# One hand-ordered schedule for block-sparse attention and a gated layer: passes of 256 queries, plain loads and DMA transposes in place of TensorE transposes

## The chip, the cores and the metric

The kernel runs on one core of one Trainium2 chip. The metric is the device time of one execution in microseconds (us), the median of three runs. Times of single instructions are from one execution taken by the hardware profiler. The engines are named as in the profile: PE is TensorE (PEld its weight loads), DVE is VectorE, ACT is ScalarE, POOL is GpSimd, SP is the queue engine that here only issues DMAs.

## The reference

Attention over 4 batches, 8 heads, 768 positions and 64 features per head, with a mask in blocks of 32 positions (24 by 24 blocks: the neighbours, the first and last rows and columns, and three sampled blocks in each row). The result, 3,072 rows of 512, goes through one layer: a product to 1,024 columns, h times softmax(h), a normalisation by mean and variance with gain, and a product back to 512 columns.

```python
scores = scale * np.matmul(q, k.transpose(0, 1, 3, 2))
...  # mask of 32 x 32 blocks, masked scores -> -1e9
attn = np.exp(scores - np.max(scores, axis=-1, keepdims=True))
attn = attn / (np.sum(attn, axis=-1, keepdims=True) + 1e-09)
x = np.matmul(attn, v)        # then (B, S, H * D) -> 3072 x 512
h = x @ w_in                  # 3072 x 1024
e = np.exp(h - np.max(h, axis=-1, keepdims=True))
solu = h * e / (np.sum(e, axis=-1, keepdims=True) + 1e-09)
mu, var = np.mean(solu, -1, keepdims=True), np.var(solu, -1, keepdims=True)
out = ((solu - mu) / np.sqrt(var + 1e-06) * g_ln) @ w_out
```

## The kernel before

**Attention.** The work goes in 16 pairs of heads. A pair has 9 units; a unit is 1,024 columns of scores (keys on the partitions, queries along the columns), which PE writes into two banks of PSUM and one ACT instruction turns into bf16 exponentials (`score_unit`). 16 times 9 gives 144 units. The mask needs no instruction of its own: `kT128` and `qT128` are 128 rows tall, 64 of them features, 24 more a factorised mask, so that the score product adds a large negative number where a block is masked. The exponentials of a pair are kept, and one pair later `out_mms` multiplies them with `vaug` (V and a column of ones, 65 columns): 72 products a pair, 8 a unit. `normalise` divides by the last column and writes `xb`, the rows of the layer's input.

**Loads and transposes.** `load_head` issues three DMAs on POOL's queue for a head, each turning fp32 into bf16 on the way. `transpose_head` brings Q and K of a head into the transposed form: 6 PE transposes into one PSUM bank, one DVE copy into `kT128` or `qT128`; two heads a pair.

**The layer.** It goes in 24 tiles of 128 rows. A tile has five steps (`moe_step`): `moe_x` (4 PE transposes, a DVE copy), `moe_h` twice (4 products of 512 columns, exponential on ACT, product and statistics on DVE), `moe_t` for the tile before (8 PE transposes, a DVE copy) and `moe_o` for the tile before (8 products, scaling on ACT, the store). One step in six is empty.

**The order.** Program order is only a priority; a scheduler places the instructions on each engine. A tile can start when all 8 heads of its batch are done, so steps are issued only from the sixth pair on (`p > PB`), one a unit. The steps left when the last pair is done run alone (the `while` loop). Transposes of Q and K, of `moe_x` and of `moe_t` share one PSUM buffer, `p_tp`. The weights are loaded at the start; `prep_w`, `prep_mean` and the subtraction fold gain and mean into `w_cen_sb`.

Of the kernel before, what the change touches and what calls it, by code (L numbers as in the profile page):

```python
# [7 lines left out]
FP32 = mybir.dt.float32  # L8
# [193 lines left out]
def kernel(  # L202
# [15 lines left out]
    NB = S // BLK  # L218
    TQ = 128
# [11 lines left out]

    nc.scalar.preload_act_table_set("natural_log_exp_and_others")

    const_pool = ctx.enter_context(tc.tile_pool(name="const", bufs=1))

    qT128 = [const_pool.tile([TQ, S], BF16, name=f"qT128_{i}") for i in range(2)]
    kT128 = [const_pool.tile([TQ, S], BF16, name=f"kT128_{i}") for i in range(2)]
    for t in qT128 + kT128:
        nc.vector.memset(t[D : TQ, :], 0.0)

    with tc.tile_pool(name="m_ps", bufs=1, space=bass.MemoryType.PSUM) as m_ps, \
         tc.tile_pool(name="m_sb", bufs=1) as m_sb:
        maskT = block_mask(nc, m_sb, m_ps, sampled_blocks, NB, NEG)

        sel = m_sb.tile([NB, NB, BLK], FP32)
        nc.vector.memset(sel, 0.0)
        nc.gpsimd.affine_select(out=sel, in_=sel, compare_op=ALU.not_equal,
                                fill=1.0, base=0, channel_multiplier=1,
                                pattern=[[-1, NB], [0, BLK]])
        for t in kT128:  # L250
            nc.vector.tensor_copy(out=t[D : D + NB, :].rearrange("p (q o) -> p q o", o=BLK),
                                  in_=sel)
        for t in qT128:
            nc.vector.tensor_copy(out=t[D : D + NB, :].rearrange("p (q o) -> p q o", o=BLK),
                                  in_=maskT.rearrange("p (q o) -> p q o", o=1).broadcast_to([NB, NB, BLK]))

    ident = const_pool.tile([128, 128], BF16)
    nc.vector.memset(ident, 0.0)
    nc.gpsimd.affine_select(out=ident, in_=ident, compare_op=ALU.not_equal,
                            fill=1.0, base=0, channel_multiplier=1,  # L260
                            pattern=[[-1, 128]])
    mean_w = const_pool.tile([128, 128], BF16)
    nc.vector.memset(mean_w, 1.0 / d_ff)


    recip_all = const_pool.tile([TQ, B * H * NCH], FP32)
    esum_all = const_pool.tile([128, n_tiles * 2], FP32)
    n_r, n_e = B * H * NCH, n_tiles * 2
# [5 lines left out]
    nc.vector.memset(ones_c, 1.0)  # L274

    w_in_sb = const_pool.tile([128, KD, d_ff], BF16)
    w_out_sb = const_pool.tile([128, KF, d_model], BF16)
    w_cen_sb = const_pool.tile([128, KF, d_model], BF16)
    g_ln_sb = const_pool.tile([128, KF], FP32)
    w_out_f = const_pool.tile([128, KF, d_model], FP32)  # L280

    work = ctx.enter_context(ExitStack())
    a_qk = work.enter_context(tc.tile_pool(name="a_qk", bufs=4))
    a_exp = work.enter_context(tc.tile_pool(name="a_exp", bufs=2))
# [4 lines left out]
    p_tp = work.enter_context(tc.tile_pool(name="p_tp", bufs=1, space=bass.MemoryType.PSUM))  # L289
    p_h = work.enter_context(tc.tile_pool(name="p_h", bufs=2, space=bass.MemoryType.PSUM))  # L290

    xbs = {}
    loads = {}

    def load_head(bi):
        b, h = bi // H, bi % H
        qc = a_qk.tile([TQ, NCH, D], BF16, tag="qc")
        kc = a_qk.tile([TQ, NCH, D], BF16, tag="kc")
        nc.gpsimd.dma_start(out=kc, in_=k[b, h, :, :].rearrange("(c p) d -> p c d", p=TQ))  # L299
        nc.gpsimd.dma_start(out=qc, in_=q[b, h, :, :].rearrange("(c p) d -> p c d", p=TQ))  # L300
        vaug = a_qk.tile([TQ, NCH, D + 1], BF16, tag="vaug")
        nc.gpsimd.dma_start(  # L302
            out=vaug[:, :, 0:D],
            in_=v[b, h, :, :].rearrange("(c p) d -> p c d", p=TQ))
        nc.vector.memset(vaug[:, :, D : D + 1], 1.0)
        loads[bi] = (qc, kc, vaug)

    def transpose_head(bi):
        qc, kc, _ = loads[bi]
        for src, dst in ((kc, kT128[bi % 2]), (qc, qT128[bi % 2])):  # L310
            tp = p_tp.tile([D, S], BF16, tag="tp")
            for c in range(NCH):
                nc.tensor.matmul(tp[:, c * TQ : (c + 1) * TQ],  # L313
                                 src[:, c, :], ident, is_transpose=True,
                                 start=(c == 0), stop=(c == NCH - 1))
            nc.vector.tensor_copy(out=dst[0:D, :], in_=tp)  # L316
# [3 lines left out]
    UNITS = 9  # L320
    exs_of = {}

    def score_unit(pair, u):
        if u == 0:
            exs_of[pair] = a_exp.tile([TQ, 2 * NCH * S], BF16, tag="exs", name=f"exs{pair}")
        sco = p_sco.tile([TQ, 2, 512], FP32, tag="sco")
        for i in range(2):
            bank = 2 * u + i
            bi = 2 * pair + bank // 9
            lo = (bank % 9) * 512  # L330
            hi = lo + 512
            c = lo
            while c < hi:
                jc = c // S
                e = min(hi, (jc + 1) * S)
                nc.tensor.matmul(sco[:, i, c - lo : e - lo],  # L336
                                 kT128[bi % 2][:, jc * TQ : (jc + 1) * TQ],
                                 qT128[bi % 2][:, c - jc * S : e - jc * S],
                                 start=(c == lo), stop=(e == hi))
                c = e  # L340
        nc.scalar.activation(out=exs_of[pair][:, u * 1024 : (u + 1) * 1024],  # L341
                             in_=sco.rearrange("p a b -> p (a b)"), func=ACT.Exp, scale=scale)

    ops_of = {}

    def out_mms(pair, i0, i1):

        for i in range(i0, i1):
            hh, jc, ic = i // 36, (i % 36) // NCH, i % NCH
            bi = 2 * pair + hh  # L350
            if i % 36 == 0:
                ops_of[bi] = p_op.tile([TQ, NCH, D + 1], FP32, tag="op", name=f"op{bi}")
            op = ops_of[bi]
            base = hh * NCH * S + jc * S + ic * TQ
            nc.tensor.matmul(op[:, ic, :], exs_of[pair][:, base : base + TQ],  # L355
                             loads[bi][2][:, jc, :],
                             start=(i % 36 == 0), stop=(i % 36 == 35),
                             skip_group_check=True)
            if i % 36 == 35:
                normalise(bi, op)  # L360

    def normalise(bi, op):
        b, h = bi // H, bi % H
        if h == 0:
            xbs[b] = a_sm.tile([TQ, NCH, H * D], BF16, tag="xb", name=f"xb{b}")
        recip = recip_all[:, bi * NCH : (bi + 1) * NCH].rearrange("p (c o) -> p c o", o=1)
        nc.vector.reciprocal(out=recip, in_=op[:, :, D : D + 1])
        nc.vector.tensor_tensor(out=xbs[b][:, :, h * D : (h + 1) * D], in0=op[:, :, 0:D],  # L368
                                in1=recip.broadcast_to([TQ, NCH, D]), op=ALU.mult)


    xTs, solus, rstds = {}, {}, {}

    def moe_x(t):
        xb = xbs[t // NCH]
        tps = p_tp.tile([128, KD, 128], BF16, tag="tp")
        for c in range(KD):
            nc.tensor.matmul(tps[:, c, :], xb[:, t % NCH, c * 128 : (c + 1) * 128],  # L378
                             ident, is_transpose=True,
                             start=(c == 0), stop=(c == KD - 1))  # L380
        xTs[t] = mo_sb.tile([128, KD, 128], BF16, tag="xT", name=f"xT{t}")
        nc.vector.tensor_copy(out=xTs[t], in_=tps)  # L382

    stats_of = {}

    def moe_h(t, i):
        xT = xTs[t]
        if i == 0:
            solus[t] = mo_sb.tile([128, d_ff], BF16, tag="solu", name=f"solu{t}")
            stats_of[t] = mo_sb.tile([128, 2, 6], FP32, tag="stats", name=f"stats{t}")  # L390
        hps = p_h.tile([128, HF], FP32, tag="h")
        for c in range(KD):
            nc.tensor.matmul(hps, xT[:, c, :], w_in_sb[:, c, i * HF : (i + 1) * HF],  # L393
                             start=(c == 0), stop=(c == KD - 1))
        e = mo_sb.tile([128, HF], BF16, tag="e")
        nc.scalar.activation(out=e, in_=hps, func=ACT.Exp, scale=1.0,  # L396
                             accum_out=esum_all[:, 2 * t + i : 2 * t + i + 1])
        so = solus[t][:, i * HF : (i + 1) * HF]
        nc.vector.tensor_mul(out=so, in0=hps, in1=e)  # L399
        nc.vector.bn_stats(out=stats_of[t][:, i, :], in_=so)  # L400
        if i == 1:
# [12 lines left out]
            nc.scalar.activation(out=rstds[t], in_=lnv, func=ACT.Exp, scale=-0.5)  # L414

    lnTs = {}

    def moe_t(t):
        tps2 = p_tp.tile([128, KF, 128], BF16, tag="tp")
        for c in range(KF):  # L420
# [135 lines left out]
```

## Time and profile before

| what | value |
|---|---|
| median of 3 runs (lowest, highest) | 303.93 us (303.35, 303.96) |
| span of the profiled execution, first to last instruction | 302.5 us |
| busy: PE, DVE, ACT, POOL | 248.4, 165.1, 195.7, 82.7 us |
| mean granted TensorE clock | 0.982 |
| HBM read, written | 23.07 MB, 6.29 MB |

The page gives no time of the profiled execution but its span, which is 1.43 us below the median of the runs; whoever adds up durations of the profile gets a span, and has to add that much for a time. "Busy" is the time in which an engine had an instruction under way. PE's instructions overlap, so its rate is read from the distance of two starts and not from the length of one instruction. In lists of groups, the number behind the x is a count, and the last part is the idle time of the engine ahead of these instructions with what ended it. The stages of the kernel are read from the view of windows, which gives the busy time of each engine in a stretch of the span.

### The profile page before, as it was taken

The numbers are of one execution on the slowest core, as the hardware profiler recorded it, in microseconds if no ns is written. First come the engines' busy times: TensorE is split into PE (matmuls) and PEld (weight loads), VectorE is DVE, ScalarE is ACT, GpSimd is POOL, SyncE is SP. The second block draws the span as 40 slices with busy tenths as digits, with TensorE's granted clock in tenths as the row PEclk, the third lists the DMA queues.
The fourth block names the chain that finished last, engine by engine and source line by source line (L and its number), as shares of the span: only waits on it lengthen the run. The fifth ranks groups of instructions, "written<-read, shape, count | busy, mean of one in ns | idle before, by whom it ended". The sixth has DMA issues, their size and how long they took to land.

```text
span 302.5 us, 6313 instructions
## 1 busy us (share of the span) xinstructions
PE 248.4 (82%) x2556; PEld 152.2 (50%) x2603; DVE 165.1 (55%) x446; ACT 195.7 (65%) x315; POOL 82.7 (27%) x110
## 2 busy tenths in 40 slices
PE   0248999998989898979989999699889987777772
PEld 0024666665655465545656655465545564333430
DVE  6263343434567356357466556547456756757770
ACT  1005999997868586838768776759857863344340
POOL 5069655543424232323333242232111000000000
PEclk9999999999999999979999999989999999999997
DMA  5989999997647664765946774756213011011002
GB/s 150 264 55 120 91 68 71 62 67 52 42 28 78 72 73 30 76 39 63 89 39 63 74 77 26 76 62 48 44 41 22 35 37 37 35 66 41 36 35 78
DMA packets 81365, 19.35 MB, mean 64 GB/s; under 512 B 76721, under 2 KB 76722, under 8 KB 81330
## 3 DMA queue, kind: packets, MB, share of 16 engines
q0 software_dynamic: 75792, 10.49, 51.1%
q1 hardware_dynamic: 5538, 8.39, 7.9%
q8 instruction: 22, 0.36, 0.5%
q14 instruction: 13, 0.11, 0.1%
HBM read 23.07 MB, written 6.29 MB: 97 GB/s over the span
## 4 chain that ended last, share of the span: by engine, by line
PE 49%; DVE 24%; ACT 12%; issue 8%; DMA 5%; POOL 1%; SPq 0%; DVEq 0%; ACTq 0%
PE sco L336 12%; PE ops L430 10%; DVE solu L399 8%; PE tp L313 8%; PE hps L393 8%; PE op L355 7%; ACT exs L341 6%; ACT e L396 5%; DVE stats L400 5%; DMA w_out_f<-in_moe_w_out_dram 4%; DVE lnT L425 3%; DVE qT L316 2%; PE tps L421 1%; PE tps L378 1%; ACT ot L433 1%
## 5 line engine op out<-in xcount | busy, mean ns | idle before, releaser
L341 ACT ACTIVATE exs<-sco 128x1024 bf16<-128x1024 f32 x144 | 141.2, 1027 | 20.8 <-PE sco L336 13.3
L336 PE MATMUL sco<-qT,kT 128*128 128x256 bf16 (+1 forms) x354 | 86.2, 331 | 2.6 <-ACT exs L341 1.1
L355 PEld LDWEIGHTS <-exs 128*128 128x128 bf16 x1152 | 52.9, 99 | 20.7 <-DVE xb L368 4.1
L355 PE MATMUL op<-vaug,exs 128*128 128x65 bf16 x1152 | 60.7, 195 | 2.1 <-issue 0.8
L430 PE MATMUL ops<-w_cen_sb,lnT 128*128 128x512 bf16 x186 | 46.9, 384 | 7.5 <-DVE lnT L425 6.0
L393 PE MATMUL hps<-w_in_sb,xT 128*128 128x512 bf16 x181 | 45.6, 380 | 5.9 <-DVE xT L382 4.4
L399 DVE TENSOR_TENSOR solu<-hps,e 128x512 bf16<-128x512 f32 x48 | 32.7, 682 | 27.2 <-ACT e L396 27.2
L299 POOL DMA_DIRECT2D kc<-in_k_dram x32 | 26.7, 833 | 75.2 <-PE tp L313 64.0
L336 PEld LDWEIGHTS <-kT 128*128 128x128 bf16 x384 | 32.0, 99 | 17.4 <-issue 4.2
L433 ACT ACTIVATE ot<-ops,rstd 128x512 f32<-128x512 f32 x24 | 16.5, 687 | 37.3 <-PE ops L430 19.8
L396 ACT ACTIVATE e<-hps 128x512 bf16<-128x512 f32 x48 | 28.8, 601 | 17.0 <-PE hps L393 16.4
L302 POOL DMA_DIRECT2D vaug<-in_v_dram x32 | 26.5, 829 | 45.4 <-PE op L355 34.3
L400 DVE BATCH_NORM_STATS2 stats<-solu 128x6 f32<-128x512 bf16 x48 | 32.9, 685 | 10.5 <-issue 6.6
L300 POOL DMA_DIRECT2D qc<-in_q_dram x32 | 26.7, 835 | 25.1 <-PE tp L313 12.1
L430 PEld LDWEIGHTS <-lnT 128*128 128x128 bf16 x192 | 16.8, 99 | 26.6 <-DVE lnT L425 9.6
L316 DVE COPY qT<-tp 64x768 bf16<-64x768 bf16 x32 | 17.3, 539 | 21.2 <-PE tp L313 19.7
L393 PEld LDWEIGHTS <-xT 128*128 128x128 bf16 x192 | 15.9, 97 | 22.0 <-DVE xT L382 7.1
L316 DVE COPY kT<-tp 64x768 bf16<-64x768 bf16 x32 | 17.3, 541 | 15.4 <-PE tp L313 8.1
L313 PE MATMUL tp<-ident,kc 128*64 128x128 bf16 x192 | 18.0, 228 | 7.7 <-DVE lnT L425 3.7
L313 PE MATMUL tp<-ident,qc 128*64 128x128 bf16 x192 | 17.4, 228 | 6.9 <-DVE kT L316 6.4
L313 PEld LDWEIGHTS <-kc 128*64 128x64 bf16 x192 | 12.8, 112 | 18.0 <-issue 16.9
L313 PEld LDWEIGHTS <-qc 128*64 128x64 bf16 x192 | 12.6, 112 | 16.9 <-issue 15.6
(62 smaller groups left out, 159.5 us busy)
## 6 DMA issues: line engine op xcount, KB each, us to landing
out_dram<-ot SPq DMA_DIRECT2D x24, 256.0 KB, 2.0
kc<-in_k_dram POOLq DMA_DIRECT2D x32, 96.0 KB, 3.0
qc<-in_q_dram POOLq DMA_DIRECT2D x32, 96.0 KB, 3.0
vaug<-in_v_dram POOLq DMA_DIRECT2D x32, 96.0 KB, 3.2
w_out_f<-in_moe_w_out_dram SPq DMA_DIRECT2D x1, 2048.0 KB, 11.0
w_in_sb<-in_moe_w_in_dram POOLq DMA_DIRECT2D x1, 1024.0 KB, 10.7
samp_i<-in_sampled_blocks_dram SPq DMA_DIRECT2D x1, 0.6 KB
g_ln_sb<-in_moe_g_ln_dram SPq DMA_DIRECT2D x1, 4.0 KB, 2.4
```

What stands on the lines that cost most here:

```text
L299: nc.gpsimd.dma_start(out=kc, in_=k[b, h, :, :].rearrange("(c p) d -> p c d", p=TQ))
L300: nc.gpsimd.dma_start(out=qc, in_=q[b, h, :, :].rearrange("(c p) d -> p c d", p=TQ))
L313: nc.tensor.matmul(tp[:, c * TQ : (c + 1) * TQ], src[:, c, :], ident, is_transpose=True, start=(c == 0), stop=(c == NCH - 1))
L316: nc.vector.tensor_copy(out=dst[0:D, :], in_=tp)
L336: nc.tensor.matmul(sco[:, i, c - lo : e - lo], kT128[bi % 2][:, jc * TQ : (jc + 1) * TQ], qT128[bi % 2][:, c - jc * S : e - jc * S], start ...
L341: nc.scalar.activation(out=exs_of[pair][:, u * 1024 : (u + 1) * 1024], in_=sco.rearrange("p a b -> p (a b)"), func=ACT.Exp, scale=scale)
L355: nc.tensor.matmul(op[:, ic, :], exs_of[pair][:, base : base + TQ], loads[bi][2][:, jc, :], start=(i % 36 == 0), stop=(i % 36 == 35), skip ...
L393: nc.tensor.matmul(hps, xT[:, c, :], w_in_sb[:, c, i * HF : (i + 1) * HF], start=(c == 0), stop=(c == KD - 1))
L396: nc.scalar.activation(out=e, in_=hps, func=ACT.Exp, scale=1.0, accum_out=esum_all[:, 2 * t + i : 2 * t + i + 1])
L399: nc.vector.tensor_mul(out=so, in0=hps, in1=e)
L400: nc.vector.bn_stats(out=stats_of[t][:, i, :], in_=so)
L430: nc.tensor.matmul(ops, lnTs[t][:, c, :], w_cen_sb[:, c, :], start=(c == 0), stop=(c == KF - 1))
```

## The change

The program is written anew between the start and the final check, inside `manual_schedule()`: the order in which instructions are written down is now the order of each engine. Every step goes into a list with a time in units (`at(when, fn, ...)`), and `emit` writes the list in the order of these times.

- A pass is 256 queries of one batch with all 8 heads: 12 passes of 12 units, again 144 units of 1,024 columns. A unit is two heads by two tiles of keys by 256 queries: 4 score products of 256 columns (before: 2 or 3 products of 512 or 256), one exponential, and 8 products with V one and a half units later.
- A pass is all that two tiles of the layer need, so the layer of a pass runs in the pass after it, cut into pieces of 2 or 3 products of 512 columns, one piece a unit.
- Rows are dealt out as `(p c)`: a partition holds 6 successive positions, so Q, K, V come in plain fp32 DMAs of two heads with 1,536 bytes in a row, issued on SP (three of the first on ACT). The cast to bf16 is an instruction of POOL (46 of 48) or DVE (2).
- The mask's 24 rows are written as columns 64 to 87 of the natural-layout tiles `kn` and `qn` once, and are transposed with them; the score product then has 88 rows instead of 128.
- Q and K of the first batch are transposed on PE (`turn_pe`, 96 transposes); of the other three by DMA (`turn_dma`: 24 DMAs of 12 blocks of 128 by 128). The layer's input (`x_turn`, 12 DMAs of 8 blocks) and its inner activation (`ln_turn`, 24 DMAs of 8 blocks) are transposed by DMA only. All are issued on SP.
- The exponential of the layer is one instruction of 1,024 columns, the inverse root is a power on POOL, the last scaling is on DVE.

```diff
-    def load_head(bi):
-        nc.gpsimd.dma_start(out=kc, in_=k[b, h, :, :].rearrange("(c p) d -> p c d", p=TQ))
...
-    def transpose_head(bi):
-    def moe_x(t):
-    def moe_t(t):
...
+    def at(when, fn, *args):
+        plan.append((when, len(plan), fn, args))
+    def emit():
+        for _, _, fn, args in sorted(plan, key=lambda x: x[:2]):
+            fn(*args)
...
+    def load(eng, src, b, pr, key):
+        st = a_st.tile([TQ, 2, NCH * D], FP32, tag="st", name=f"st_{key}{b}_{pr}")
+        eng.dma_start(out=st, in_=src[b, 2 * pr : 2 * pr + 2].rearrange(
+            "h (p c) d -> p h (c d)", c=NCH))
+    def turn_dma(b, pr, key):
+        src, dst = (kn, KT[b % 2]) if key == "k" else (qn, QT[b % 2])
+        nc.sync.dma_start_transpose(
+            out=dst[:, 2 * NCH * pr : 2 * NCH * (pr + 1), :],
+            in_=src[:, 2 * pr : 2 * pr + 2].rearrange("p h c e -> p (h c e)"))
...
+    def x_turn(ps):
+        xT_of[ps] = mo_sb.tile([128, PC * KD, 128], BF16, tag="xT", name=f"xT{ps}")
+        nc.sync.dma_start_transpose(out=xT_of[ps],
+                                    in_=xb_of.pop(ps).rearrange("p c m -> p (c m)"))
+    def ln_turn(ps, i):
+        lnT_of[ps, i] = mo_sb.tile([128, KF, 128], BF16, tag="lnT", name=f"lnT{t}")
+        nc.sync.dma_start_transpose(out=lnT_of[ps, i], in_=solu_of[ps, i])
...
+    with tc.manual_schedule():
...
+        for s in range(n_units):
+            at(s, exps, s)
+            at(s + 1.5, outs, s)
+            if s + 2 < n_units:
+                at(s + 0.8, scores, s + 2)
+            if u == UP - 1:
+                at(s + 1.55, normalise, ps, pr)
+        for b in range(1, B):
+            s0 = SLOTS * NPB * (b - 1) + (14 if b == 1 else 2)
...
+                    at(s0 + 1.5 * n, load, nc.sync, src, b, pr, key)
+                    at(s0 + 1.5 * n + 3.0, cast, nc.gpsimd, b, pr, key)
+                    if key != "v":
+                        at(s0 + 1.5 * n + 4.5, turn_dma, b, pr, key)
+        for ps in range(NPASS):
+            b0 = SLOTS * (ps + 1)
+            at(b0 + 0.6, x_turn, ps)
+            for i in range(PC):
+                hs = b0 + 3 + 6 * i
+                at(hs + 0.1, h_mms, ps, i, 0, 3)
+                at(hs + 1.1, h_mms, ps, i, 3, 6)
+                at(hs + 2.1, h_mms, ps, i, 6, 8)
+                at(hs + 2.95, e_exp, ps, i)
+                at(hs + 3.9, solu, ps, i)
+                at(hs + 3.92, ln_turn, ps, i)
+                at(hs + 4.0, stats, ps, i)
+                at(hs + 5.0, rstd, ps, i)
+                os = hs + 9
+                at(os + 0.1, o_mms, ps, i, 0, 3)
+                at(os + 1.1, o_mms, ps, i, 3, 6)
+                at(os + 2.1, o_mms, ps, i, 6, 8)
+                at(os + 2.9, store, ps, i)
```

More of the change, by code (lines that the diff above doesn't have):

```diff
@@ L230 @@
     n_tiles = n_tok // 128
+    KR = D + NB
+    PC = 2
+    QW = PC * TQ
+    NPB = NCH // PC
+    NPASS = B * NPB
+    NP = H // 2
+    UP = NCH // 2
+    SLOTS = NP * UP
     nc.scalar.preload_act_table_set("natural_log_exp_and_others")
     const_pool = ctx.enter_context(tc.tile_pool(name="const", bufs=1))
[L236 to L255, printed above, removed]
     ident = const_pool.tile([128, 128], BF16)
[L258 to L261, printed above, removed]
     mean_w = const_pool.tile([128, 128], BF16)
[L263 to L268, printed above, removed]
+    n_r, n_e = NPASS * NP * 4, n_tiles
+    recip_all = const_pool.tile([TQ, n_r], FP32)
+    esum_all = const_pool.tile([128, n_tiles], FP32)
     okr = const_pool.tile([128, n_r + n_e], FP32)
@@ L323, in score_unit @@
-    def score_unit(pair, u):
-        if u == 0:
[L325 to L360, printed above, removed]
```

455 lines of the change are left out of this document (296 added, 159 removed).

## The prediction

> **What bounds the kernel now.** I read the page first (busy times, slices, chain), then the windows, then the timeline of PE, then the groups.
>
> ```profile
> PE 248.4 (82%) x2556; PEld 152.2 (50%) x2603; DVE 165.1 (55%) x446; ACT 195.7 (65%) x315; POOL 82.7 (27%) x110
> PE   0248999998989898979989999699889987777772
> ACT  1005999997868586838768776759857863344340
> ```
>
> PE is nearly always busy from the fifth slice on, but ACT is full only in slices 5 to 9, and PE falls to 7 and below in the last seven. So there are stages. I cut the span at the first exponential, at the first step of the layer, and at the end of the last attention exponential:
>
> ```profile
> 24.94 1.94 ACT L341 ACTIVATE exs<-sco 128x1024 bf16<-128x1024 f32 x2 [6.29 <-PE sco L336]
> ...
> 245.95 1.02 ACT L341 ACTIVATE exs<-sco 128x1024 bf16<-128x1024 f32 x1
> ```
>
> ```profile
> 0.00:24.90 24.90, 6.64 (x25) 3.13 (x26) 13.49 (x40) 2.08 (x3) 11.31 (x24) 1.00 0.92 153
> 24.90:67.20 42.30, 41.29 (x505) 26.91 (x513) 16.19 (x44) 40.77 (x44) 26.02 (x33) 1.00 1.23 79
> 67.20:247.00 179.80, 162.99 (x1743) 102.14 (x1772) 101.28 (x271) 134.00 (x215) 45.39 (x56) 0.98 0.55 54
> 247.00:302.50 55.50, 37.51 (x294) 20.02 (x297) 34.13 (x93) 18.88 (x55) 0.00 (x0) 0.97 0.12 45
> ```
>
> Columns: length, then busy time of PE, PEld, DVE, ACT, POOL, the granted clock, DMA share, GB/s. A head of 24.9 us with hardly any product; 42.3 us of attention alone (45 of the 144 units), ACT full; 179.8 us of 99 units with one layer step each, 1.816 us a unit; a tail of 55.5 us in which layer tiles run one behind the other. The distance of two stores' scalings in the tail is one tile, 5.83 us:
>
> ```profile
> 264.23 0.69 ACT L433 ACTIVATE ot<-ops,rstd 128x512 f32<-128x512 f32 x1 [2.50 <-issue]
> ...
> 270.06 0.69 ACT L433 ACTIVATE ot<-ops,rstd 128x512 f32<-128x512 f32 x1 [2.50 <-issue]
> ```
>
> **PE's prices**, from the distance of starts in its timeline:
>
> ```profile
> 160.90 0.52 PE L313 MATMUL tp<-ident,kc 128*64 128x128 bf16 x6
> 161.36 0.42 PE L355 MATMUL op<-vaug,exs 128*128 128x65 bf16 x8
> 161.61 0.59 PE L336 MATMUL sco<-qT,kT 128*128 128x512 bf16 x2
> 162.04 0.41 PE L355 MATMUL op<-vaug,exs 128*128 128x65 bf16 x8
> ...
> 164.31 0.61 PE L421 MATMUL tps<-ident,solu 128*128 128x128 bf16 x8 [0.19 <-DVE qT L316]
> 164.75 0.60 PE L336 MATMUL sco<-qT,kT 128*128 128x512 bf16 x3
> ...
> 165.70 1.90 PE L430 MATMUL ops<-w_cen_sb,lnT 128*128 128x512 bf16 x8
> 167.44 0.39 PE L378 MATMUL tps<-ident,xb 128*128 128x128 bf16 x4
> ```
>
> Six transposes of Q or K take 0.46 us (77 ns each), eight products with V 0.25 (31 ns), one unit's scores 0.43, eight transposes of the layer 0.44 (55 ns), eight products of 512 columns 1.74 (0.217). A unit of the 99 holds 0.43 + 0.25 + 24/9 x 0.077 + 2 x 0.055 + 24/9 x 0.217 = 1.58 us. It takes 1.816, so 0.24 is waiting. In that stage PE is the bound; the transposes are 0.315 of it.
>
> **PE after the change.** A unit keeps its scores (1,024 columns; now four products with a weight load each, where a load with a 65-column product takes 31 ns altogether, so a load hides under 108 ns of columns; 88 rows instead of 128 I price at nothing, the columns being as many), its 8 products with V, and 32/12 products of the layer: 0.44 + 0.25 + 0.58 = 1.27 us, 15.2 a pass. All transposes but 96 leave PE, and with them the DVE copies and the one PSUM buffer that three kinds shared.
>
> **The other engines as the next bound.**
>
> ```profile
> 29.23 31.17 ACT L341 ACTIVATE exs<-sco 128x1024 bf16<-128x1024 f32 x33 [0.73 <-PE sco L336]
> ```
>
> ```profile
> L341 ACT ACTIVATE exs<-sco 128x1024 bf16<-128x1024 f32 x144 | 141.2, 1027 | 20.8 <-PE sco L336 13.3 <-PE tp L313 6.8
> L396 ACT ACTIVATION_READ_ACCUMULATOR e<-hps 128x1 f32 x48 | 9.6, 200 | 0.0
> L399 DVE TENSOR_TENSOR solu<-hps,e 128x512 bf16<-128x512 f32 x48 | 32.7, 682 | 27.2 <-ACT e L396 27.2
> L368 DVE TENSOR_TENSOR xb<-op,recip_all 128x384 bf16<-128x384 f32 x32 | 17.7, 554 | 0.8
> L433 ACT ACTIVATE ot<-ops,rstd 128x512 f32<-128x512 f32 x24 | 16.5, 687 | 37.3 <-PE ops L430 19.8 <-issue 17.5
> L247 POOL TENSOR_SCALAR_AFFINE_SELECT sel<-sel 24x768 f32<-24x768 f32 x1 | 1.0, 987 | 0.7 <-DVE ident L258 0.7
> ```
>
> Undisturbed, 33 exponentials take 31.17 us: 0.945 each. ACT then has 12 x 0.945 + 2 x (1.03 + 0.20) = 13.8 us a pass, below 15.2: it follows PE, with 1.4 to spare. DVE takes over the scaling (at most the 16.5 us of ACT) and loses its copies; even without losing them it would have 182 us. POOL loses its DMA issues and gets 46 casts of 768 columns. The nearest row is the select of 768 columns, 0.99 us: 46 us in all, hidden as long as a cast is ready 1.5 units before its transpose; at double the price still hidden, since the next batch is loaded a batch ahead.
>
> **The DMA transposes** appear in no trace of before, and they decide. 36 + 24 DMAs move 24 x 12 + 36 x 8 = 576 blocks of 128 x 128 bf16, all on SP's queue with 45 loads and 24 stores. Nearest rows:
>
> ```profile
> q0 software_dynamic: 75792, 10.49, 51.1%
> q1 hardware_dynamic: 5538, 8.39, 7.9%
> ...
> out_dram<-ot SPq DMA_DIRECT2D x24, 256.0 KB, 2.0
> w_out_f<-in_moe_w_out_dram SPq DMA_DIRECT2D x1, 2048.0 KB, 11.0
> ```
>
> A packet of q0 costs 302.5 x 16 x 0.511 / 75,792 = 32.6 ns for 138 bytes on average, one of q1 69 ns for 1,515 bytes. Lower bound: a transpose is an ordinary copy of 256 KB, 2.0 us from issue to landing like the store. Upper bound of the rows: 138 bytes a packet, 0.48 us a block over 16 engines, 3.9 + 2.0 = 5.9 us. I take rows of 256 bytes (one row of a block) at q0's price: 128 x 32.6 ns / 16 = 0.26 us a block, 2.1 + 2.0 = 4.1 us for 8 blocks. It lies between the ends and is nearest to small packets, which a transpose has to cut.
>
> Against these rows stands a rule: the Trainium skill, in "VectorE: DVE Perf Modes", § The three transpose paths, puts a 128 x 128 block at 1309 ns by DMA and 390 ns on TensorE; the trace disagrees with the second, with 55 ns in a stream, and cannot show the first. The Trainium skill, in "DMA: Bandwidth & Descriptors", § Latency and other measured facts, measured 261 GB/s for DMA transposes, an estimated 0.126 us a block; by this page the sum below would be about 235.
>
> Where the landing counts: `x_turn` follows the last `normalise` of a pass, and the layer's first product stands in PE's fixed order at b0 + 3.1. Between that pass's last products and it PE has three units of scores, two of products with V and two pieces of the layer: 3 x 0.44 + 2 x 0.25 + 5 x 0.217 = 2.9 us. `normalise` takes some 0.9 of that (L368 and its reciprocal). So 2.0 us of cover, and PE stands 2.1 us a pass; behind it wait products with V and scores, then ACT. On SP, loads and transposes of the next batch wait behind `x_turn`, and nobody needs them within 14 units. `ln_turn` has four units or more (5 us): hidden. The long exponential of the layer delays the next unit's by 1.23 us, of which ACT's spare time and the second score buffer take most: 0 to 1.23, I take 0.3, twice a pass. Pass: 15.2 + 2.1 + 0.6 = 17.9 us, or 1.49 a unit; the present 0.24 us of waiting a unit would give 1.51, about the same.
>
> **Head.** Now the mask is done at 15.26 and K's load leaves at 17.52:
>
> ```profile
> 15.26 0.17 DVE L53 TENSOR_TENSOR maskT<-maskT,anyeq 24x24 f32<-24x24 f32 x1
> ...
> 17.52 0.84 POOL L299 DMA_DIRECT2D kc<-in_k_dram  x1 [10.17 <-DVE w_out_sb L451]
> ...
> 20.62 0.82 PE L313 MATMUL tp<-ident,kc 128*64 128x128 bf16 x6 [2.59 <-DMA kc<-in_k_dram]
> ```
>
> Both came late behind the weights. After: Q and K of two heads, 0.8 MB, at w_out's rate (2 MB in 11 us) land by 6 us. The mask's selects (two of 768 columns and ten short ones), memsets and factors take an estimated 11.7; then 4.3 us from transpose to first exponential as now (20.62 to 24.94): 16. Bounds: 6 + 4.3 = 10, and 24.9 as now.
>
> **First pass,** without a layer: ACT's pace, 12 x 0.945 = 11.3, and 1.2 for late transposes: 12.5. Top: 12 x 1.8 = 22.
>
> **Tail,** one pass of the layer alone, after the last exponential: products with V and `normalise` 0.9, transpose 4.1, h 1.74, exponential 1.23, product with e 2 x 0.68 = 1.36, the same three for the second tile (one h buffer) 4.33, transpose 4.1, out 1.74, scaling 0.68, store 2.3: 22.5 us. It was 55.5.
>
> **Sum:** 16 + 12.5 + 11 x 17.9 + 22.5 = 248; 302.5 becomes 248. The runs' median is 1.4 above the span, so 249.
>
> **The rivals.**
> *Transposes like ordinary copies* (2.0 us): no wait for `x_turn`, 15.8 a pass, tail 18.3: 16 + 12.5 + 174 + 18.3 + 1.4 = 222. For it: the store's 2.0. Against: small pieces. Chance 0.22.
> *Landing of about 6 us and over*, queueing included: 3.9 us of standing, 19.7 a pass, tail 26: 273, up to 300 where `x_turn` waits behind loads or turns of the next batch. Chance 0.15.
> *SP's queue becomes the bound; slower.* A pass brings 48 blocks and on average 5.9 us of loads and stores (48 loads of 256 packets and 4,150 packets of stores at 69 ns over 16 engines). At 0.48 us a block that is 29 us a pass, 11 x 29 + 51 + 1.4 = 373. It decides from (302.5 - 51) / 11 = 22.9 us a pass, 0.35 us a block. For it: 0.26 is not far below, and already gives the DMA engines 18.4 us a pass, as much as a pass lasts. Against: a transpose whose packets carry more than 256 bytes is far from it. By the Trainium skill's 1309 ns ("VectorE: DVE Perf Modes", § The three transpose paths), block after block, an estimated 754 us in transposes alone. Chance 0.19.
> *The change doesn't do what it says*: the transposes moved but PE's fixed order gives back as waits what they took, 1.8 us a unit: 51 + 132 x 1.8 + 1.4 = 290, and 308 with head and first pass at their tops; it alone can end within 0.2% of now (about what a measurement of this kernel can tell). Chance of that 0.01.
>
> **How the numbers follow.** The forecast's own case has 0.43 and reaches from 235 to 262. Faster in all but the third rival and the equal case: 0.80; same 0.01; slower 0.19. The range goes from the copy-like case, 222, to 303, which leaves out the slower case and little below.
>
> **What would show it.** Right: about 60 transposes on SP landing in 3 to 5 us; PE waiting about 2 us for `x_turn` once a pass and for nothing else as long; the distance of 12 exponentials about 18 us; the first exponential near 16; about 22 us after the last. Wrong: DMA engines busy all along with SP's transposes landing in over 8 us (queue bound), PE waiting for casts of POOL or for `normalise` in every group, or an ACT that is full (then PE's prices were too high).

## The result and the profile after

The changed kernel takes 278.89 us (median of 5 runs, 275.16 to 282.94) against 303.96 before (303.35 to 304.99), a ratio of 0.9095 (95% interval 0.9039 to 0.9151; the ratio is of the undisturbed runs, 275.16 to 278.89). It is faster by 9 per cent, where the forecast's own case, 249.0, was 18; its range, 222 to 303, holds the result, the 235 to 262 of its own case does not. The profiled execution has a span of 276.8 us; the prediction's sum for the span was 248.

From the page: busy times, slices of PE, of the granted clock and of the DMA engines, the hardware queue, and the chain by engine.

```profile
span 276.8 us, 5494 instructions
PE 211.5 (76%) x2191; PEld 143.7 (52%) x2224; DVE 134.4 (49%) x317; ACT 169.2 (61%) x195; POOL 63.8 (23%) x100
PE   0699795768989519969989907997989989895752
PEclk9999999968999956997999975999999999999997
DMA  7799587999899999980369999993351233553441
...
q1 hardware_dynamic: 93460, 44.97, 70.0%
...
PE 45%; DMA 23%; DVE 12%; ACT 8%; SPq 4%; issue 4%; POOL 2%; POOLq 0%; DVEq 0%; ACTq 0%
```

PE lost 36.9 us of busy time, but its slices have two holes in mid-kernel (a 1 and a 0) where there were none before. At each hole and in the slice behind it the granted clock falls to 5 to 7 tenths. Around each hole the DMA engines stand at 9 for several slices; before they had 0.55 in this stage. DMA now carries 23 per cent of the chain.

The waits of PE, with total, count and longest:

```profile
PE h L406 <- DMA xT<-xb: 29.4, 12, 8.3
PE sco L349 <- ACT exs L360: 9.8, 20, 0.5
...
PE o L455 <- DMA lnT<-solu: 4.9, 4, 2.5
PE op L373 <- DVE xb L387: 3.1, 2, 2.4
```

One wait dominates, the layer's first product for `x_turn`: 29.4 us in 12 passes, but 8.3 us in the worst. It is not one constant a pass. So the passes have to be looked at one by one. Cut at every twelfth exponential, the passes from the second on take 20.3, 22.9, 17.2, 27.8, 20.4, 17.2, 27.3, 18.0, 17.1, 17.2 and 15.4 us. The first pass, four of these and the tail in the view of windows (columns as in the prediction):

```profile
13.90:29.80 15.90, 15.32 (x208) 13.35 (x207) 8.27 (x18) 11.80 (x12) 7.24 (x11) 1.00 1.02 281
...
73.00:90.20 17.20, 15.20 (x172) 10.49 (x173) 9.45 (x22) 13.81 (x19) 3.81 (x6) 1.00 0.91 185
90.20:118.00 27.80, 18.34 (x176) 12.18 (x180) 9.47 (x22) 13.92 (x18) 8.18 (x11) 0.82 1.14 264
118.00:138.40 20.40, 17.14 (x175) 11.55 (x177) 9.47 (x22) 13.81 (x18) 1.09 (x2) 0.92 0.40 74
...
200.90:218.00 17.10, 15.52 (x175) 10.84 (x177) 9.47 (x22) 13.84 (x18) 1.10 (x2) 1.00 0.33 78
...
250.60:276.80 26.20, 13.28 (x67) 5.22 (x65) 13.90 (x33) 3.34 (x6) 1.64 (x3) 0.91 0.35 91
```

The row from 200.9 is the pass as it was forecast: no loads, PE busy 15.52 us of 17.10. The row from 90.2 does the same work for PE and ACT in 27.80 us. It is a pass in which the next batch is loaded (POOL has 11 instructions, nearly all casts), the DMA share is 1.14, and the clock 0.82. The next row has no loads left (share 0.40) and is long all the same, with the clock at 0.92; the experiment without loads comes back to it.

The stages together: the 144 units took 42.3 + 179.8 = 222.1 us before and take 15.9 + 220.8 = 236.7 now, though 20 of the 24 tiles of the layer end in them instead of 15. The head is 11.0 us shorter and the tail 29.3. So the whole gain stands in the head and the tail; the stage in which the transposes were to be saved, which the prediction put at 209.4, became longer.

What happened at the start of the long pass, in the order of SP's queue, and PE's row behind it:

```profile
91.88 2.55 SPq L312 DMA_TRANSPOSE KT<-kn  x1
94.48 0.58 SPq L297 DMA_DIRECT2D st_k<-in_k_dram  x1
95.35 1.68 SPq L312 DMA_TRANSPOSE QT<-qn  x1
97.08 0.57 SPq L297 DMA_DIRECT2D st_q<-in_q_dram  x1
97.75 2.29 SPq L398 DMA_TRANSPOSE xT<-xb  x1
100.14 1.63 SPq L426 DMA_TRANSPOSE lnT<-solu  x1
...
102.95 1.46 PE L406 MATMUL h<-w_in_sb,xT 128*128 128x512 bf16 x3 [8.13 <-DMA xT<-xb]
```

`normalise` ended at 92.60, but SP was busy until 97.65 with two transposes and two loads for the next batch, which nobody needs for many units. `x_turn` left 5.15 us late; its first product came another 5.21 us later, where a quiet pass has 0.03 and 3.27. PE stood for 8.13 us. Then it ran at half clock: three products of 512 columns took 1.46 us, where the same three take 0.81 to 0.82 at full clock.

```profile
97.90:108.00 10.10, 5.04 (x30) 2.96 (x31) 0.60 (x2) 1.02 (x1) 2.99 (x4) 0.50 1.14 252
```

By the clock's records in the trace, half clock lasted 6.8, 10.2, 3.4 and 10.2 us in the four stretches between the first pass and the tail. The Trainium skill, in "TensorE: Matmul & The Clock Gate", Part 1, says that PE's clock falls to half after an idle window of 3,413 ns and comes back after a busy one; the four durations are one, two and three such windows, so the trace agrees in the lengths. It also shows that such a window need not be idle throughout. The stretches of half clock start at 56.85, 97.81, 125.12, 162.66 and 268.48, whole multiples of 3.413 us apart. Three stretches of that length, the first two right before half clock:

```profile
94.40:97.81 3.41, 0.42 (x4) 0.13 (x2) 1.76 (x6) 1.44 (x2) 1.66 (x2) 1.00 1.12 291
121.70:125.12 3.42, 1.37 (x16) 0.72 (x15) 1.08 (x4) 1.45 (x2) 0.55 (x1) 1.00 1.11 161
251.41:254.82 3.41, 1.80 (x15) 0.84 (x14) 2.36 (x5) 0.56 (x2) 0.00 (x0) 1.00 0.17 34
```

PE was busy 1.37 of 3.42 us in the second, with one wait of 2.05, and the clock fell; it was busy 1.80 of 3.41 in the third, and the clock stayed, though a wait of 3.08 us (253.21 to 256.30) began there. Laid over this trace from its first clock record on, the windows at full clock with PE busy for at most 0.40 of them are followed by half clock, those with 0.53 or more are not.

The landings (median us from issue to landing):

```profile
out_dram<-ot SPq DMA_DIRECT2D x24, 256.0 KB, 2.6
...
lnT<-solu SPq DMA_TRANSPOSE x24, 3.5
xT<-xb SPq DMA_TRANSPOSE x12, 3.2
KT<-kn SPq DMA_TRANSPOSE x12, 5.0
QT<-qn SPq DMA_TRANSPOSE x12, 5.0
```

### The profile page after: what moved, and what is told of

It reads as the page before. It is cut to its first block, busy times and chain, and to the rows that moved or that the text cites. A ratio compares the mean times of both kernels' runs of the same rounds, so it can differ in the third digit from the quotient of the medians.

```text
span 276.8 us, 5494 instructions
## 1 busy us (share of the span) xinstructions
PE 211.5 (76%) x2191; PEld 143.7 (52%) x2224; DVE 134.4 (49%) x317; ACT 169.2 (61%) x195; POOL 63.8 (23%) x100
## 2 busy tenths in 40 slices
DMA packets 94834, 47.60 MB, mean 172 GB/s; under 512 B 77908, under 2 KB 90196, under 8 KB 94804
## 4 chain that ended last, share of the span: by engine, by line
PE 45%; DMA 23%; DVE 12%; ACT 8%; SPq 4%; issue 4%; POOL 2%; POOLq 0%; DVEq 0%; ACTq 0%
DMA xT<-xb 15%; PE h L406 14%; PE sco L349 14%; PE op L373 8%; PE o L455 7%; ACT e L413 4%; ACT exs L360 4%; DMA st_v<-in_v_dram 3%; DVE solu L419 3%; DMA lnT<-solu 3%; SPq L312 2%; DVE stats L433 2%; DMA st_q<-in_q_dram 2%; PE tp_q L323 1%; DVE xb L387 1%
## 5 line engine op out<-in xcount | busy, mean ns | idle before, releaser
L349 PE MATMUL sco<-QT,KT 88*128 88x256 bf16 x576 | 91.8, 283 | 10.8 <-ACT exs L360 9.8
L406 PE MATMUL h<-w_in_sb,xT 128*128 128x512 bf16 x170 | 54.9, 412 | 31.5 <-DMA xT<-xb 29.4
L373 PE MATMUL op<-VA,exs 128*128 128x65 bf16 x1152 | 61.6, 197 | 3.1 <-DVE xb L387 3.1
L349 PEld LDWEIGHTS <-KT 88*128 88x128 bf16 x576 | 50.3, 101 | 18.7 <-issue 13.5
L455 PE MATMUL o<-w_cen_sb,lnT 128*128 128x512 bf16 x181 | 51.2, 389 | 5.6 <-DMA lnT<-solu 4.9
L413 ACT ACTIVATE e<-h 128x1024 bf16<-128x1024 f32 x24 | 24.6, 1023 | 33.3 <-PE h L406 33.3
L448 POOL TENSOR_TENSOR rstd<-vpe,mhalf 128x1 f32<-128x1 f32 x24 | 13.3, 553 | 120.8 <-DVE vpe L441 120.7
L419 DVE TENSOR_TENSOR solu<-h,e 128x1024 bf16<-128x1024 f32 x24 | 29.1, 1214 | 3.4 <-ACT e L413 3.4
L387 DVE TENSOR_TENSOR xb<-op,recip_all 128x256 bf16<-128x256 f32 x48 | 20.4, 424 | 1.7
L308 POOL CAST kn<-st_k 128x768 bf16<-128x768 f32 x15 | 12.7, 848 | 35.8 <-DMA st_k<-in_k_dram 35.8
L461 DVE TENSOR_SCALAR ot<-o,rstd 128x512 f32<-128x512 f32 x24 | 18.0, 750 | 3.1 <-PE o L455 3.1
L308 POOL CAST qn<-st_q 128x768 bf16<-128x768 f32 x15 | 12.4, 825 | 24.4 <-DMA st_q<-in_q_dram 23.9
```

Source lines behind the costliest of these rows:

```text
L308: eng.tensor_copy(out=o, in_=i)
L349: nc.tensor.matmul(sco[:, hh, kk * QW : (kk + 1) * QW], KT[b % 2][0:KR, h * NCH + 2 * u + kk, :], QT[b % 2][0:KR, h * NCH + PC * j : h * N ...
L373: nc.tensor.matmul(op[:, hh, ic, :], exs[:, u, hh, kk, ic * TQ : (ic + 1) * TQ], VA[b % 2][:, 2 * pr + hh, 2 * u + kk, :], start=(u == 0 a ...
L387: nc.vector.tensor_tensor(out=xb_of[ps][:, :, 2 * pr * D : 2 * (pr + 1) * D].rearrange("p c (h d) -> p h c d", h=2), in0=op[:, :, :, 0:D], ...
L406: nc.tensor.matmul(h_of[ps, i][:, half, :], xT_of[ps][:, i * KD + c, :], w_in_sb[:, c, half * HF : (half + 1) * HF], start=(c == 0), stop= ...
L413: nc.scalar.activation(out=e_of[ps, i], in_=h_of[ps, i].rearrange("p a b -> p (a b)"), func=ACT.Exp, scale=1.0, accum_out=esum_all[:, t : ...
```

## The experiments

All times are medians beside runs of the kernel before on the same chip (302.14, 301.48, 302.34 and 304.12 in the four groups), so ratios carry across groups, microseconds only roughly. Diffs are against the changed kernel, where nothing else is said. Where an expectation names a span, the measured time less some 2 us is to be compared with it (1.4 to 2.7 in these runs). Theory A is that the order on SP's queue alone makes `x_turn` late; theories B and C, that the next batch's DMA work, put down in half of its time, is too much for the queue and the engines there; D and E are about the clock.

**Three units more of cover.** The layer's pieces start at unit 6 of a pass and not 3.

```diff
-                hs = b0 + 3 + 6 * i
+                hs = b0 + 6 + 6 * i
```

> The layer of a pass starts three units later (hs = b0 + 6), nothing else changes; the transposed rows of the layer's input get about 3.8 us more before PE needs them. Theory A (the wait for them on SP's queue, and the half clock after it, hold the missing time): PE's waits for xT fall from 29 us to under 8, the passes of 27.8 and 27.3 us fall to 18 to 20, the clock stays at 1.0, span 250 to 257. Theory B (the DMA engines are full in these passes, so more cover only moves the wait): passes 2, 4 and 7 stay over 22 us, waits turn up at lnT or K, span 266 to 274.

Measured: 262.91, ratio 0.8706 (0.8646 to 0.8767), between the two ranges. Most passes without loads take 16.6 us and their wait is gone. The loading passes stay long, 22.4, 25.9 and 25.2 us. In the middle one SP is again busy without a pause, and `x_turn` leaves 8.7 us after `normalise` (the row of DVE):

```profile
86.00 4.12 SPq L312 DMA_TRANSPOSE KT<-kn  x1
86.01 0.42 DVE L387 TENSOR_TENSOR xb<-op,recip_all 128x256 bf16<-128x256 f32 x1
90.17 0.57 SPq L297 DMA_DIRECT2D st_k<-in_k_dram  x1
90.84 0.42 SPq L463 DMA_DIRECT2D out_dram<-ot  x1
91.36 3.01 SPq L312 DMA_TRANSPOSE QT<-qn  x1
...
95.09 1.24 SPq L398 DMA_TRANSPOSE xT<-xb  x1
...
99.34 1.03 PE L406 MATMUL h<-w_in_sb,xT 128*128 128x512 bf16 x2 [2.83 <-DMA xT<-xb]
```

The delay is no constant of the transfer. It grows with what stands in front: one transpose of 12 blocks holds SP for 4.12 us here.

**Without the DMA transposes of K and Q** (the first batch's K and Q are used again).

```diff
-                    if key != "v":
-                        at(s0 + 1.5 * n + 4.5, turn_dma, b, pr, key)
```

> The 24 DMA transposes of Q and K of batches 1 to 3 are left out (the first batch's K and Q are used for all batches, so the result is another); their loads and casts stay. Theory A in its form 'x_turn stands behind turns that wait for casts': xT waits under 8 us in all, no half clock, span 244 to 250. If the loads alone do it (A': their landing and their place on the queue), passes 4 and 7 stay over 23 us, span 262 to 270.

**Without the loads as well.**

> Loads, casts and transposes of Q, K and V for batches 1 to 3 are left out (the first batch is used for all, so the result is another). Both theories: every pass from the second on takes 17.1 to 17.9 us as the undisturbed ones do, span 241 to 246; this is the whole of what the next batch's loading costs (31 to 36 us). Above 255 there is a further cause that has nothing to do with the loading.

Measured: 252.60, ratio 0.8334 (0.8275 to 0.8393), and 250.18, 0.8270 (0.8226 to 0.8314); the first lies at the upper end of its range, the second 2 to 3 us over its own. The 24 transposes cost 0.0761 of 302, some 23 us; the 36 loads and their casts about 2 more, which the intervals don't separate. All of the next batch's loading is thus some 25 us, less than the 31 to 36 expected. Without the transposes `x_turn` leaves 0.03 us after `normalise` in every pass; the longest wait is 2.9 us. The first of the two kernels also gives the price of a transpose, by its packets of the hardware queue beside those of the changed kernel:

```profile
span 254.5 us, 5505 instructions
...
q1 hardware_dynamic: 55828, 35.53, 54.5%
```

16 x (276.8 x 0.700 - 254.5 x 0.545) us over 37,632 packets fewer are 23.4 ns a packet. The 128 packets of a block are 0.19 us of 16 engines.

In the kernel without loads most passes take 17.1 or 17.2 us, but the sixth still 20.4 and the ninth 18.1, as in the changed kernel (20.4 and 18.0). So the sixth pass is not long for the loads. In both kernels `x_turn` leaves on time in these passes and its first product comes 4.1 to 4.9 us after its issue instead of 3.2 to 3.4. In all four cases one packet of 16 KB of the queue that the page calls `instruction` moves among the transposes' packets, and 16 to 20 of these take over 1 us, where the median is 18 ns; the `x_turn` of the other quiet passes has no such packet among its own. Here the sixth pass of the kernel without loads, from the issue of `x_turn` to its first product (101.7 to 106.7; packets, MB, share of 16 engines):

```profile
q1 hardware_dynamic: 1859, 0.47, 86.0%
q8 instruction: 1, 0.02, 1.6%
```

No experiment moved that packet, so that it is the cause is likely, not shown.

**`x_turn` ahead of the loads and turns** that stand less than 2.6 units before it.

```diff
+        def clear(w):
+            m = SLOTS * round(w / SLOTS)
+            return m + 0.65 if m - 2.6 < w <= m + 0.6 else w
...
+                    tl = clear(s0 + 1.5 * n)
+                    at(tl, load, nc.sync, src, b, pr, key)
```

> Loads and turns of the next batch that stand in the last 2.6 units ahead of x_turn on SP's queue are placed right behind it. Theory A: x_turn leaves within 1.5 us of normalise in all passes, PE's longest wait for xT falls from 8.3 to 2 to 4 us, span 260 to 267. Theory B: it leaves in time but lands in over 5 us, the longest wait stays over 5, span 270 to 277.

```profile
PE o L455 <- DMA lnT<-solu: 19.9, 8, 5.0
PE h L406 <- DMA xT<-xb: 14.0, 12, 2.9
```

Measured: 277.59, ratio 0.9200 (0.9147 to 0.9254), no gain. The edit did what it says: `x_turn` leaves 0.03 us after `normalise` in all 12 passes and its waits fall from 29.4 to 14.0. But the waits for `ln_turn` rise from 4.9 to 19.9. The work put behind `x_turn` now stands in front of `ln_turn`. Theory A in this form has fallen: a better order moves the wait. The span lies in theory B's range, but not for B's reason: the longest wait for `x_turn` is 2.9 us and not over 5.

**Loads further apart**: 2.75 units instead of 1.5 (1.9 for the second batch, which starts late).

```diff
+            dn = 1.9 if b == 1 else 2.75
-                    at(s0 + 1.5 * n, load, nc.sync, src, b, pr, key)
+                    at(s0 + dn * n, load, nc.sync, src, b, pr, key)
```

> The 12 loads, casts and 8 turns of the next batch are spread over 33 units of the batch instead of 18 (2.75 units apart instead of 1.5; for the second batch 1.9). Nothing is left out. Theory C (the DMA engines are over full in the stretch of 18 units, share 1.13 to 1.14, and half empty in the rest): passes 2, 4 and 7 fall from 23 to 28 us to 17 to 20, the passes without loading now rise by at most 1, no DMA share over 1 in any pass, span 250 to 257. Theory A (the order on SP's queue): turns now stand in front of x_turn in more passes, waits stay, span 264 to 274.

Measured: 267.53, ratio 0.8848 (0.8785 to 0.8912), in theory A's range, and the DMA share still reaches 1.15. But the waits for `x_turn` fall from 29.4 to 21.3 us and it leaves at most 2.34 us late, where A had them stay: what is left is mostly late landing, in the median 4.0 us after issue instead of 3.2. One pass still takes 24.7 us, with a wait of 5.03, but the other loading passes 17.6 to 20.8. Neither theory is borne out alone.

**Both: loads further apart and three units of cover.**

> The spreading of the run before and the layer three units later together. Theory C: what is left of the waits for xT after spreading is covered as well, passes of 16.6 to 17.5 us, span 241 to 248. Theory A: as the later layer alone, 258 to 264.

```profile
80.20:101.30 21.10, 17.18 (x175) 11.36 (x177) 10.49 (x26) 14.08 (x16) 5.16 (x7) 0.92 1.09 234
101.30:117.90 16.60, 15.38 (x175) 10.94 (x177) 8.73 (x21) 13.87 (x17) 4.36 (x6) 1.00 1.10 242
...
134.50:151.40 16.90, 15.40 (x175) 10.80 (x177) 9.03 (x22) 13.99 (x17) 4.37 (x6) 1.00 1.15 263
```

```profile
PE o L455 <- DMA lnT<-solu: 8.5, 10, 2.0
...
PE h L406 <- DMA xT<-xb: 2.0, 2, 1.1
```

Measured: 244.80, ratio 0.8119 (0.8086 to 0.8153), within theory C's range (two passes of 18.5 and 21.1 us are over what C said of passes), and better than both parts added: the ratio falls by 0.0976, where the parts alone give 0.0389 and 0.0247. Work and bytes are those of the changed kernel. The DMA share is 1.10 to 1.15 in passes of 16.6 and 16.9 us, as high as in the pass of 27.8. So full DMA engines alone don't make a pass long. In this kernel `x_turn` still leaves up to 3.16 us late and lands up to 5.5 us after its issue; the three more units cover it. Spread, the delay is short enough for the cover; crammed, it outgrows it (the first experiment). The kernel even beats the one without any loading (0.8270): the cover also takes the quiet passes' wait away, and they take 16.6 us instead of 17.1. In the 21.1 us pass 3.4 us lie at half clock.

**The next batch's loads on POOL's queue.**

```diff
-                    at(s0 + 1.5 * n, load, nc.sync, src, b, pr, key)
+                    at(s0 + 1.5 * n, load, nc.gpsimd, src, b, pr, key)
```

> The loads of batches 1 to 3 are issued on POOL's queue instead of SP's, at the same places; bytes, casts and turns are the same. Theory A (order on SP's queue): x_turn and the turns no longer stand behind loads, span 258 to 268. Theory C (full engines): the same packets in the same stretch, passes 4 and 7 stay over 24 us, span 270 to 280.

Measured: 290.70, ratio 0.9583 (0.9513 to 0.9653): both ranges missed, it is slower than the changed kernel. SP has 36 DMAs fewer, but its transposes of K and Q land after 6.4 and 7.4 us instead of 5.0, and the waits for `ln_turn` rise to 13.8 us. SP's own instructions aren't what is short. The Trainium skill, in "DMA: Bandwidth & Descriptors", § Issuing engines are not separate DMA queues, says that DMAs of all issuing engines run on the same 16 DMA engines and that another issuer saves only issue time; the trace agrees that nothing is won. The DMA engines have more to do: the two queues' packets take 74.8% of 289.9 us here, 217 us, and 72.0% of 276.8 in the changed kernel, 199. Whether that is where the 12 us went isn't settled.

**The layer's input transposed on PE**, with a copy by ACT; the other transposes as changed.

```diff
-            at(b0 + 0.6, x_turn, ps)
+            at(b0 + 2.2, x_turn_pe, ps)
```

> x_turn is done by PE (8 transposes into the layer's PSUM buffer, one ACT copy) instead of a DMA; all else as it was. If the landing of x_turn alone is the trouble: no pass over 20 us, span 248 to 258. Theory C: one sixth of the transposed blocks leaves the full stretch, but lnT is then the next late transfer, its waits rise from 5 to 10 us or more, span 260 to 270. Undisturbed passes take 17.0 to 18.0 us (0.44 us more on PE, no landing).

Measured: 264.31, ratio 0.8798 (0.8747 to 0.8848). An undisturbed pass takes 17.6 us, half a microsecond more. Of the excess of the long passes, part is left: waits for `ln_turn` are 12.0 us now, and one pass takes 23.8. These are theory C's signs, and the median lies in its range. With a sixth of the transposed blocks back on PE the kernel is faster than the changed one.

**PE kept at work during the two long waits.**

```diff
+            if i == 0 and ps in (3, 6):
+                for _ in range(36):
+                    nc.tensor.matmul(h_of[ps, i][:, 0, :], w_in_sb[:, 0, 0:128],
+                                     w_in_sb[:, 0, 0:512], start=True, stop=True)
```

> What it changes: in the passes that begin with the fourth and the seventh, 36 products of 512 columns whose result nobody reads stand in PE's order just ahead of the layer's first product, so PE has 7.8 us of work (36 x 0.217) while it would otherwise stand 8.13 and 8.26 us for the layer's transposed input. Everything else is as in the changed kernel (278.89). Theory D (the half clock after PE's long waits is a cost of its own, some 5 us behind each of the two waits: 97.8 to 108.1 and 162.7 to 172.9 at half speed): the granted clock stays full in these two passes, they take 22 to 25 us instead of 27.8 and 27.3, in all 269 to 274. Theory E (the half clock hides behind the next transposes, which are late anyway): the passes stay at 27 us, in all 277 to 281. If the filler only begins late, because it stands behind other waiting products, it adds up to 2 us.

The second half of such a pass, from the layer's first product to the pass's end, in the changed kernel and then in this one:

```profile
102.95:118.00 15.05, 14.41 (x133) 9.56 (x136) 5.34 (x13) 8.96 (x12) 3.77 (x5) 0.83 1.15 255
167.97:182.90 14.93, 14.30 (x133) 9.49 (x136) 5.34 (x13) 8.93 (x11) 3.77 (x5) 0.83 1.17 255
```

```profile
102.35:115.00 12.65, 12.01 (x134) 8.45 (x135) 5.34 (x13) 9.01 (x12) 3.77 (x5) 1.00 1.21 274
```

Measured: 271.37, in the range of theory D. The same 133 or 134 products take 12.65 us at full clock instead of 15.05 at 0.83, with the DMA engines just as full: 2.4 us of such a pass were the half clock's own (2.5 in the other one). The two passes take 24.4 and 24.3 us instead of 27.8 and 27.3; the rest is that the layer's first product came 1.0 and 0.4 us earlier in its pass. In the whole, the ratio 0.9023 (0.8945 to 0.9101) overlaps that of the changed kernel (0.9095), so the total gain isn't separated from none.

**The end of the best version.** First with two of the last pass's transposes on PE:

> What it changes: the spread loads and the three units of more cover together (244.8 before in that form), and in the last pass, where PE has nothing else to do, the layer's input and the last tile's inner activation are turned on PE (8 transposes of 55 ns and one ACT copy of about 1.0 us, 1.5 us in all) instead of by DMA (3.1 us from issue to the first product that uses it, twice). If the tail is a chain of latencies, each turn gains about 1.5 us: 240.5 to 243.5. If the ACT copy or PE's order gives it back: 244 to 246.

```profile
PE o L478 <- DVE ot L484: 2.7, 1, 2.7
...
PE o L478 <- ACT xT_last L410: 1.1, 1, 1.1
```

Measured: 247.31, ratio 0.8225 (0.8166 to 0.8285), over both ranges; the tail takes 28.8 us and not 26.3. The transposed x stands in the one PSUM buffer that the layer's output uses, so the output's products of the tile before wait 1.1 us for ACT's copy, which is part of the 2.5. And at the last tile PE waits 2.7 us for that buffer with either kind of transpose: the DMA had not been the last thing there. Then with DVE's summaries ahead of the last scaling, and the version without either once more beside it (the diff is against that version):

```diff
-        at(last + 5.0, check_r)
-        at(last + 6 + 6 + 7.0, check_e)
+        at(SLOTS * NPASS + 2.5, check_r)
+        at(last + 6.0, check_e)
```

> What it changes: the spread loads and the three units of more cover together (244.8 in that form), and the two small summaries of DVE at the end (of the divisors and of the exponentials' sums, whose result the program reads before it ends) are written ahead of the last scaling instead of behind it. In that kernel the last summary ended at 239.55 and the span at 244.08, so 4.5 us follow it; the last store was issued at 238.24. If the end hangs on the summary, it moves up until the last store's landing (2.6 us behind its issue) is the end: 1.5 to 3 us less, 242 to 243.5. If the end hangs on the store and what follows it: 244 to 245.5.

> What it changes: the spread loads and the three units of more cover together, once more, beside the kernel with the summaries moved, on one chip. Expected 244 to 246, a ratio of 0.809 to 0.815 to the kernel before; the kernel with PE turns at the end (247.31, ratio 0.8225) then lost about 1 per cent, because its end hangs on the one buffer for the layer's output and not on the turns.

Measured: 243.71, ratio 0.8028 (0.7983 to 0.8072), and 245.92, 0.8105 (0.8064 to 0.8146). In the profiles 4.4 us follow the last scaling's end with the summaries ahead of it, and 5.9 without. The first time lies between its two ranges, the second in its own. The medians say 2.2 us less; the intervals overlap by a little, so this gain is likely rather than shown.

## Why the prediction was right, and where not

The direction was right, and a pass without disturbance is what was worked out: 17.1 us, with PE busy for 15.5. The value fell short by 30 us, and the gain is less than half of the one forecast, 25 of 55 us. That the transposes' move made the gain isn't shown: the 144 units, with five more tiles of the layer in them, became 14.6 us longer where 12.7 less were forecast, and it is head and tail that bring it all. No run keeps the transposes of Q and K on PE in the new order; the one that puts the layer's input back on PE is faster than the changed kernel (264.31). By its steps:

- **PE's raw pass, 15.2 us:** the row from 200.9 has 15.52 us busy. Right. ACT has 13.84 against 13.8.
- **Head, 16 us:** the first exponential came at 13.9, 2.1 earlier; within the bounds.
- **First pass, 12.5 us:** 15.9. PE, not ACT, was the bound there: PE is busy for 15.32 of it. The late transposes of K and Q were run there, the first of them slowly: six took 0.80 to 0.84 us up to 19.3, where the trace's clock records begin, with full clock, and 0.50 behind it. That the clock had not come up is inferred.
- **Tail, 22.5 us:** 26.2, with 3.4 us of it at half clock and the last 1.5 as well.
- **A DMA transpose, 0.26 us a block and 4.1 us of landing:** the kind was right (256-byte packets: the page counts 77,908 packets under 512 bytes, of which 576 x 128 = 73,728 would be the transposes), the price too high: 0.19 us a block, and 3.2 us in the median from issue to landing. The rival with an ordinary copy's 2.0 us and the slower one with 0.35 us a block both fell.
- **PE stands 2.1 us a pass for `x_turn`, 17.9 us a pass:** this term was mis-sized, on both sides. In a quiet pass the wait is 0.36 to 0.43 us and the pass 17.1: `x_turn` is some 3.2 us on its way and has 2.9 of cover, not 4.1 and 2.0. In passes with loads the wait is up to 8.3. The 11 passes took 220.8 instead of 197: 23.9 of the 28.8 us that the span missed; head, first pass and tail make the rest (-2.1 + 3.4 + 3.7).
- **"On SP, loads and transposes of the next batch wait behind `x_turn`":** this is the sentence that failed, and with it the term. The rows show the reverse: `x_turn` waits behind them, 1.95, 5.15 and 5.65 us in three passes, and lands later too. The step asked who waits for the moved DMA, and not for whom it waits. The prediction held the other case only as a rival's top: "19.7 a pass, tail 26: 273, up to 300 where `x_turn` waits behind loads or turns of the next batch", chance 0.15. What that top said came true, with 278.89. The rest of the rival did not: no landing of about 6 us (3.2 in the median), no even 19.7 a pass.
- **SP's load as an average, 18.4 us of engine time a pass:** the plan puts a batch's 12 loads and 8 transposes of 12 blocks into about 18 of 36 units, and the average hid this. Spread over more units, with three units of cover, the same work gives 244.8. That this is close to the forecast of 249 is not the forecast come true: the kernel that was forecast has neither.
- **`ln_turn` hidden:** yes in the changed kernel, with 4.9 us of waits in all. Its cover is not free, though: as soon as `x_turn` is moved forward, it is the next late one (19.9 us).
- **Half clock around long waits** was in no step. Against 17.1 us in every pass but the last, the passes have 34 us too much: 220.8 - 10 x 17.1 - 15.4. Waits for `x_turn` beyond 0.4 a pass are 22 of it, for `ln_turn` 1.0 (the other 3.9 lie in the tail), for `normalise` 3.1; about 8 remain, of which the experiment with filled waits assigns 2.4 and 2.5 to the half clock of two passes; the other two stretches of half clock lie in other passes.

What stays open: why the loads from POOL's queue cost 12 us, and what exactly holds SP for 4.12 us in one transpose; and what the new order would take with the transposes of Q and K left on PE.

## What to carry to other kernels

Price a DMA by the queue it stands in at that moment: list what is issued on the same queue in the units before it, and not the average over a pass. When a transfer is late, moving it forward in a full queue makes the next transfer late; spread what is not urgent, and give the urgent one cover for its delay under load, not for its quiet latency. A wait of PE can cost a second time, in the clock: here those of 2.05, 3.25, 8.13 and 8.26 us did, one of 3.08 did not, and it hung on how much of a 3.4-us window PE was busy.

## What was new about the hardware

- A DMA transpose of 8 blocks of 128 x 128 bf16 takes 3.2 us (`x_turn`) and 3.5 us (`ln_turn`) from issue to landing in the median, and holds SP for 1.24 us when undisturbed; one of 12 blocks held SP for 1.68 to 4.12 us in the rows above.
- Each of the two 8-us waits of PE went with 10.2 us of half clock, which began 3 us into the wait and lasted 5 us beyond it; filling the waits with unused products kept the clock up and gave 2.4 us a wait back.
- The clock went to half at multiples of 3.413 us, behind windows of that length at full clock in which PE was busy for at most 0.40 of the time, and not behind those with 0.53 or more. A wait of 2.05 us inside one window was enough; one of 3.08 us on both sides of a boundary was not.
- `x_turn` came 0.8 to 1.7 us later in the quiet passes where a 16 KB packet of the `instruction` queue moved beside it.
- A DMA share above 1 (1.10 to 1.15) is no sign of a stall by itself: it stood in passes of 16.6 and of 27.8 us alike.
